# A chunked scan feeding routed experts on one core: TensorE's work of a pair regrouped by form of product, decays brought to C's rows by DMA, routing steps dealt out

## The chip, the cores and the metric

The kernel runs on one core of a Trainium2 chip. The metric is the time of one launch on the device in microseconds (us); lower is better. All arithmetic is 32-bit floating point, partly in TensorE's format fp32r.

## What is computed

Three layers follow each other; y below stands for what one hands to the next.

```python
# 1. a scan over the sequence: batch 4, 8 heads, 768 positions, 32 values, state of 16, in chunks
CB = einsum('bhin,bhjn->bhij', C, B); L = exp(cum_i - cum_j), lower triangle     # cum: running sum of log a
y  = einsum('bhij,bhjd->bhid', CB * L, x) + einsum('bhin,bhnd->bhid', C, state) * exp(cum_i)
state = exp(sum log a) * state + sum_j B_j x_j * exp(cum_end - cum_j)
# 2. routed experts on the rows y (4 x 768 rows of 256, 8 experts of 256 -> 1024 -> 256)
logits = y @ w_gate; fresh = argmax(logits); local = sigmoid(y @ w_local)
e[s] = fresh[s] if s == 0 or local[s] < 0.5 else e[s - 1]        # a recurrence along the sequence
out = softmax(logits)[e] * (relu(y @ w1[e]) @ w2[e])
# 3. a mixer: real part of a 2-D Fourier transform, a residual, a norm, and one more such layer
u = out + real(fft2(out)); result = u + relu(norm(u) @ w_ch1) @ w_ch2
```

## The kernel before

The scan lies in phase_a. The sequence is cut into six chunks of 128 positions, and each chunk into two pairs: a pair is two of the four batches with all eight heads. So the loop over `pairs` makes twelve turns, and a turn i holds parts of pairs i - 1, i and i + 1. The rows of C (ct), transposed B (bt), B (bn) and x of a chunk come by four DMAs in load.

Per pair TensorE makes: scores (L327, g), B's rows against C's rows times the decays, eight products of 128 x 256 whose weights take 32 partitions; the small products of outputs (L355, yps), sixteen with 32 columns of weights each (masked scores times x); the carries (L350, yps), four 128 x 128 products of the state with C's rows; the state's increment (L371, dps) in state_mm; and in rows four transposing products (L409, tl) that turn the pair's result back and take the gate's logits along. Before a chunk's first pair, spread (L258, eb) copies the decays of the heads to the 16 rows of each head by four products with a constant matrix bsel; VectorE then multiplies them into C's rows (ce, L262).

VectorE multiplies the scores by the causal mask (mt, L336: four instructions of 128 x 512 per pair, since a tile g holds one batch and its four banks half used) and dps by a block mask (sn, L380). ScalarE copies finished results from PSUM (x1t, L362 in keep; scr, L412 in rows), scales the state (L396) and C's rows for the scores (ch, L306 in prep). POOL, the GpSimd engine, adds the old state (sn, L386 in state_add), scales x (xt, L314 in prep_x), writes token numbers (L475), and issues the indirect DMAs that scatter finished rows to their experts' places in DRAM (L531 in leave, one for each batch of a chunk).

routing (L414 on) is the gate for a chunk: some 30 small VectorE steps with three short stays on TensorE and ScalarE. It is a generator. Each `yield` ends a step, and three calls put its steps into the order of the engines: gap(n) puts up to n VectorE steps at that place, place(0) and place(1) put the parts that need TensorE. The order is that of the code, since the scheduler is off (`tc.manual_schedule()`); an engine runs its instructions strictly in that order. A chunk's routing is entered once both pairs' rows exist.

Buffers in PSUM: g one tile of four banks, y one bank, m one bank, and the name "t" two banks, which eb, dps and tl take in turn.

In turns 6 to 9 of the loop, the weights of expert 0 are split into two parts: a quarter per turn, ScalarE rounding (L149), VectorE (384 columns) and POOL (640) subtracting (L151, w1l and w2l). load_w issues the loads, which wait on SP for the two raw buffers. After the loop come the last routing, the remaining scatters, the counts and then the experts, the first of which reads its rows (xn) back from DRAM.

## Time and profile before

| what | us |
|---|---|
| three runs | 512.03, 512.13, 513.86 |
| median | 512.13 |
| the profiled execution | 510.82 |
| its span in the profile (first to last instruction) | 509.0 |
| TensorE busy in it | 476.9 (94%) |
| VectorE, POOL, ScalarE busy in it | 276.0, 208.5, 193.0 |
| mean granted clock of TensorE, as a share of full speed | 0.955 |

The span is cut into stretches below: for each, the time that an engine was busy in it and in brackets its instructions, then the granted clock (PEclk, 1.00 is 2.4 GHz, 0.50 is 1.2 GHz), then the mean busy share of the 16 DMA engines and what they moved. In a timeline a row is an instruction or several alike in succession: its start, its length, engine, line of the code, operation, output and inputs by the program's names, and in square brackets how long the engine stood idle before it and on whom it waited. PEld is the loading of weights into TensorE, which goes on beside products. On a chain of waits the rows follow each other in time, each with the stretch of it that set the end.

### The profile page before, as it was taken

Reading aid. Unit: us, or ns where it says so; the run is one execution under the profiler, and the core shown is the slowest. Engines: PE = TensorE matmul, PEld = TensorE weight load, DVE = VectorE, ACT = ScalarE, POOL = GpSimd, SP = SyncE. Lnnn points to the kernel's source line nnn. Section 1 sums busy time; section 2 is a strip of 40 time slices with the busy share of each in tenths; the row PEclk is TensorE's granted clock in tenths of the full one; section 3 lists DMA queues with packets and bytes.
Section 4 is the critical chain, followed back from the end, with each engine's and each line's share of the span. In section 5 each row is a group of like instructions: output and inputs, shape, how many; then the busy total and the mean of one; then the engine's idle time right before and its main releaser. Section 6 shows DMA issues by size and latency. Waiting matters only on the chain.

```text
span 509.0 us, 8586 instructions
## 1 busy us (share of the span) xinstructions
PE 476.9 (94%) x3283; PEld 395.5 (78%) x3283; DVE 276.0 (54%) x695; ACT 193.0 (38%) x391; POOL 208.5 (41%) x214
## 2 busy tenths in 40 slices
PE   7899896886799999999999999798999999999997
PEld 3666563553588989898988989366998989898987
DVE  4566567663364546536363533198554757574341
ACT  2344251530355454635545542124333243443130
POOL 2223463746137575573748454274530343220000
PEclk8999795985899999999999999799999999999999
DMA  8967402132215444535445400440032201000001
GB/s 304 248 196 257 133 23 104 45 126 85 85 57 200 153 149 146 170 124 168 132 144 190 144 26 31 152 151 21 1 96 81 95 1 43 1 30 14 31 12 41
DMA packets 33553, 53.55 MB, mean 105 GB/s; under 512 B 3357, under 2 KB 24189, under 8 KB 33504
## 3 DMA queue, kind: packets, MB, share of 16 engines
q1 hardware_dynamic: 30176, 45.13, 27.8%
q0 software_dynamic: 3072, 7.46, 4.2%
q8 instruction: 28, 0.46, 0.4%
q10 hardware_dynamic: 256, 0.34, 0.2%
q14 instruction: 21, 0.17, 0.1%
HBM read 41.19 MB, written 12.77 MB: 106 GB/s over the span
## 4 chain that ended last, share of the span: by engine, by line
PE 80%; DVE 6%; DMA 5%; POOL 3%; issue 3%; ACT 2%; SPq 0%; POOLq 0%; ACTq 0%; DVEq 0%
PE mm L688 30%; PE mm L697 29%; PE yps L355 3%; PE yps L350 3%; PE dps L371 3%; PE g L327 2%; PE tp L709 2%; PE tl L409 2%; PE f L920 2%; DVE ac L492 1%; DVE mt L336 1%; DMA xs_buf<-scr,si 1%; DMA ca<-in_wg_dram 1%; DMA y_tok<-y,ids 1%; DMA z<-y_tok 1%
## 5 line engine op out<-in xcount | busy, mean ns | idle before, releaser
L690 DVE SCALAR_TENSOR_TENSOR hl<-mm,hh 128x512 fp32r<-128x512 f32 x112 | 77.0, 690 | 76.4 <-ACT hh L689 76.4
L689 ACT ACTIVATE hh<-mm 128x512 fp32r<-128x512 f32 x112 | 66.5, 596 | 92.2 <-PE mm L688 92.2
L697 PE MATMUL mm<-w2h,hh 128*128 128x256 f32 x256 | 71.9, 281 | 0.0
L697 PE MATMUL mm<-w2l,hh 128*128 128x256 f32 x256 | 71.3, 279 | 0.0
L697 PE MATMUL mm<-w2h,hl 128*128 128x256 f32 x256 | 71.3, 279 | 0.0
L737 POOL DMA_INDIRECT y_tok<-y,ids x32 | 34.5, 1078 | 52.9 <-ACT y L736 49.4
L697 PE MATMUL mm<-c2h,hh 128*128 128x256 f32 x192 | 54.4, 284 | 0.0
L697 PE MATMUL mm<-c2h,hl 128*128 128x256 f32 x192 | 53.8, 280 | 0.0
L697 PE MATMUL mm<-c2l,hh 128*128 128x256 f32 x192 | 53.8, 280 | 0.0
L688 PE MATMUL mm<-xh,w1h 128*128 128x512 f32 x128 | 51.3, 401 | 0.5 <-ACT xh L711 0.3
L688 PE MATMUL mm<-xh,w1l 128*128 128x512 f32 x128 | 51.1, 399 | 0.0
L151 POOL TENSOR_TENSOR w1l<-r,w1h 128x640 fp32r<-128x640 f32 x16 | 30.3, 1893 | 45.5 <-ACT w1h L149 45.5
L697 PEld LDWEIGHTS mm<-w2l,hh 128*128 128x128 f32 x256 | 48.3, 189 | 0.0
L697 PEld LDWEIGHTS mm<-w2h,hh 128*128 128x128 f32 x256 | 48.2, 188 | 0.0
L697 PEld LDWEIGHTS mm<-w2h,hl 128*128 128x128 f32 x256 | 48.2, 188 | 0.0
L336 DVE TENSOR_TENSOR mt<-g,ca 128x512 f32<-128x512 f32 x48 | 31.7, 684 | 16.7 <-PE g L327 16.7
L688 PE MATMUL mm<-xl,w1h 128*128 128x512 f32 x128 | 40.5, 398 | 0.0
L688 PE MATMUL mm<-xh,c1h 128*128 128x512 f32 x96 | 39.5, 411 | 0.6 <-ACT xh L711 0.6
L688 PE MATMUL mm<-xh,c1l 128*128 128x512 f32 x96 | 38.0, 396 | 0.0
L697 PEld LDWEIGHTS mm<-c2l,hh 128*128 128x128 f32 x192 | 36.2, 188 | 0.1
L697 PEld LDWEIGHTS mm<-c2h,hh 128*128 128x128 f32 x192 | 36.2, 188 | 0.1
L697 PEld LDWEIGHTS mm<-c2h,hl 128*128 128x128 f32 x192 | 36.2, 188 | 0.0
(301 smaller groups left out, 940.2 us busy)
## 6 DMA issues: line engine op xcount, KB each, us to landing
r<-in_w_dram SPq DMA_DIRECT2D x16, 1024.0 KB, 5.5
xn<-xs_buf SPq DMA_DIRECT2D x8, 530.0 KB, 6.7
rawc<-in_wc_dram SPq DMA_DIRECT2D x8, 512.0 KB, 3.7
out_dram<-o SPq DMA_DIRECT2D x24, 128.0 KB, 1.7
z<-y_tok SPq DMA_DIRECT2D x3, 768.0 KB, 6.0
xs_buf<-scr SPq DMA_DIRECT2D x8, 265.0 KB, 10.1
c1h<-in_x_dram SPq DMA_DIRECT2D x4, 512.0 KB, 5.8
xk<-y_tok SPq DMA_DIRECT2D x4, 512.0 KB, 6.8
```

The lines of the kernel that those rows point to most:

```text
L151: eng.tensor_tensor(out=l_[:, x:y], in0=r_[:, x:y], in1=h[:, x:y], op=ALU.subtract)
L327: PE.matmul(out=gp[:, q, 0, :], lhsT=bt[r:r + 32, :], rhs=ch[r:r + 32, u].rearrange("p q i -> p (q i)"), start=True, stop=True,)
L336: V.tensor_tensor(out=m[:, 2 * q:2 * q + 4, :].rearrange("p (b h) i -> p b h i", b=2), in0=gp[:, q:q + 2, 0, :].rearrange("p b (h i) -> p ...
L350: PE.matmul(out=yps[:, u, g, :], lhsT=s_st[bp][:, u, 128 * g:128 * g + 128], rhs=ops[i][0][:, u, :], start=True, stop=False, skip_group_ch ...
L355: PE.matmul(out=yps[32 * h:32 * h + 32, u, g, :], lhsT=xt[:, u, 4 * g + h, :], rhs=m[:, 4 * g + h, :], start=(c == 0), stop=True, skip_gro ...
L371: PE.matmul(out=dps[:, u, :], lhsT=lds[c]["bn"][:, 2 * bp + u, :], rhs=xts[i][:, u], start=True, stop=True)
L409: PE.matmul(out=tl[:, 137 * g:137 * g + 137], lhsT=x1t[:, u, g, :], rhs=ca[:, o:o + 137], start=True, stop=True)
L688: PE.matmul(out=ps, lhsT=w[:, d, f * 128:(f + 1) * 128], rhs=x[:, d, :], start=(k == 0), stop=(k == 5))
L689: A.activation(out=hh[:, f, :], in_=ps, func=ACTF.Relu)
L690: V.scalar_tensor_tensor(out=hl[:, f, :], in0=ps, scalar=0.0, in1=hh[:, f, :], op0=ALU.max, op1=ALU.subtract)
L697: PE.matmul(out=ps, lhsT=h[:, f, t * 128:(t + 1) * 128], rhs=w[:, f, :], start=(k == 0), stop=(k == 23))
L737: w = G.indirect_dma_start(out=y_tok, out_offset=bass.IndirectOffsetOnAxis(ap=ids[:, t:t + 1], axis=0), in_=y, in_offset=None, bounds_chec ...
```

## The change

Six things are changed in phase_a; the experts and the mixer stay as they are.

1. A turn of the loop is written in another order. scores(i + 1) makes all eight products of the next pair, into four tiles g0 to g3 of a bank each (full banks, both batches in one). Then come the sixteen small products of pair i (intra), dps of pair i + 1, the four tl of pair i, and the four carries of pair i + 1, which now open the bank y a turn ahead.
2. VectorE's four masks belong to the next pair, with up to three routing steps behind each (gap(3)), and four more at the turn's end. A chunk's routing may go on in turns of the next one: two entries in `route` ("n", "a") let a routing wait in its generator until its predecessor has set the running expert and the running counts.
3. The decays e_r are written to a DRAM tile e_d once, and for chunks 1 to 5 eight DMAs on SP's queue (load_eb, one for each head) read them back, each to 16 partitions. Of spread's work only a product remains, on POOL. Chunk 0 keeps the products of TensorE (spread0).
4. The constants ca are two tiles, ca and cb; bsel is cut to 32 rows; the two small loads of the gate's weights move from SP to ScalarE's queue; the first loads are reordered; one warming product more ahead and two behind the columns.
5. Ahead of the loop both prep and prep_x run for pairs 0 and 1, and pair 0's state. After the loop all routings still open are stepped in turn, with the scatters between.
6. load_w(1), the loads of expert 1's weights, is called in turn 10 of the scan instead of ahead of the experts.

```diff
-            warm(3)
-            A.dma_start(out=ca[:, 0:CA1], in_=io["ca"][:, 0:CA1])
+            warm(4)
+            A.dma_start(out=ca, in_=io["ca"][:, 0:CA1])
...
-            load(0)
+            load(0, ("ct", "x"))
+            A.dma_start(out=ca[:, CA["w0"][0]:CA["w0"][0] + 9], in_=io["wg"][0:128, :])
+            A.dma_start(out=ca[:, CA["w1"][0]:CA["w1"][0] + 9], in_=io["wg"][128:256, :])
+            load(0, ("bt", "bn"))
+            SP.dma_start(out=cb, in_=io["ca"][:, CA1:CAW])
...
+            def load_eb(c):
+                ebs[c] = ld.tile([128, NB, 128], FP32, tag="eb", name="eb")
+                for h in range(NH):
+                    SP.dma_start(
+                        out=ebs[c][16 * h:16 * h + 16],
+                        in_=e_d[c * NB:(c + 1) * NB, h, :].unsqueeze(0).to_broadcast([16, NB, 128]),
                     )
+
+            def spread(c):
                 ces[c] = wk.tile([128, NB, 128], FP32, tag="ce", name="ce")
-                V.tensor_tensor(out=ces[c], in0=ps0, in1=lds[c]["ct"], op=ALU.mult)
+                G.tensor_tensor(out=ces[c], in0=ebs[c], in1=lds[c]["ct"], op=ALU.mult)
...
+                gp = [pg.tile([128, 2, 2, 128], FP32, tag=f"g{q}", name=f"g{q}") for q in range(4)]
+                for u in range(2):
+                    for q in range(4):
+                        r = 32 * q
+                        PE.matmul(
+                            out=gp[q][:, u].rearrange("p h i -> p (h i)"), lhsT=lds[c]["bt"][r:r + 32, 2 * bp + u, :],
+                            rhs=ch[r:r + 32, u].rearrange("p q i -> p (q i)"), start=True, stop=True,
+                        )
...
                 yield "first"
+                while route["n"] < c:
+                    yield "first"
...
+                while route["a"] != (c, b0):
+                    yield
                 ac = route["acc"]
...
             decays()
+            SP.dma_start(out=e_d.rearrange("(s u) h i -> (u h) s i", s=2), in_=e_r[:, :, 0:128])
+            columns()
+            spread0()
+            warm(2)
+            prep(0)
+            prep_x(0)
+            prep(1)
+            prep_x(1)
+            scores(0)
             load(1)
+            load_eb(1)
             load(2)
+            load_eb(2)
             zfill(0)
             zfill(4)
...
             mask(0, 0)
             kappa0()
+            kappa()
+            state_up(0, state_mm(0))
+            carry(0)
+            spread(1)

             for i, (c, bp) in enumerate(pairs):
+                now[0] += 1
+                more = i + 1 < NP
                 if bp == 0 and c and c + 2 < NC:
                     load(c + 2)
+                    load_eb(c + 2)
+                if i in (4, 10):
+                    ws = load_w(i // 10)
...
+                if more:
+                    scores(i + 1)
+                    mask(i + 1, 3)
+                else:
+                    gap(10)
+                intra(i)
+                keep(i)
                 if i + 2 < NP:
                     prep(i + 2)
                 place(0)
+                state_add(i)
+                if more and pairs[i + 1][0] + 1 < NC:
+                    state_up(i + 1, state_mm(i + 1))
+                rows(i)
+                state_scale(i)
+                if c + 1 == NC:
+                    route_(c, 2 * bp, 2)
+                elif bp:
+                    route_(c, 0, NB)
+                gap(4)
+                place(1)
+                if more:
+                    carry(i + 1)
                 leave()
+                if bp == 1 and c + 2 < NC:
+                    spread(c + 2)
                 if i + 2 < NP:
                     prep_x(i + 2)
                 leave()
                 if 6 <= i <= 9:
                     next(ws, None)

+            while rq:
+                for r in sorted(rq, key=lambda q: q[2]):
+                    step(r)
                 leave(0)
             while scq:
                 leave(0)
```

TensorE's order in one turn, that of chunk 2's first pair (turn 4). In the rows below g are scores, eb the spread of the decays, tl the transposing products, rp the routing's, yps from ce and scr the carries and yps from mt and xt the small products, dps the state's increment. Before:

```order
L327 MATMUL g<-ch,c2h 128x256 x4
L258 MATMUL eb<-e_r,bsel 128x128 x4
L409 MATMUL tl<-ca,x1t 128x137 x4
L497 MATMUL rp<-oh,ca 128x32
L498 MATMUL rp<-ac,ca 128x32
L350 MATMUL yps<-ce,scr 128x128
L355 MATMUL yps<-mt,xt 32x128 x4
L350 MATMUL yps<-ce,scr 128x128
L355 MATMUL yps<-mt,xt 32x128 x4
L327 MATMUL g<-ch,c2h 128x256 x4
L371 MATMUL dps<-xt,c2l 128x256 x2
L350 MATMUL yps<-ce,scr 128x128
```

After (the lines have moved: L343 scores, L376 small products, L393 dps, L431 tl, L365 carries; the numbers in g_558 and the like only keep the tiles apart):

```order
L343 MATMUL g_558<-ch,c2h 128x256
L343 MATMUL g_559<-ch,c2h 128x256
L343 MATMUL g_560<-ch,c2h 128x256
L343 MATMUL g_561<-ch,c2h 128x256
L376 MATMUL yps<-mt,xt 32x128 x16
L474 MATMUL rp<-ca,kd 4x128 x2
L393 MATMUL dps<-xt,c2l 128x256 x2
L431 MATMUL tl<-ca,x1t 128x137 x4
L495 MATMUL rp<-ca,er 128x4
L365 MATMUL yps<-ce,scr 128x128 x4
```

The sixteen small products stand in one row of sixteen, and the carries in one of four, where they stood in alternation; the products eb are gone; the state's product stands ahead of the tl.

VectorE's order in the same turn; mt are the masks, sn the state's increment, and the other small names (rk, kd, si, ls, sx, cand, ex, ff, px) steps of the routing. Before:

```order
L336 TENSOR_TENSOR mt<-g,ca 128x512
L511 TENSOR_REDUCE rk<-ro 128x4
L427 TENSOR_SCALAR kd<-lg 128x4
L515 TENSOR_TENSOR si<-base,rk 128x4
L430 TENSOR_TENSOR ls<-lg,mx 128x32
L336 TENSOR_TENSOR mt<-g,ca 128x512
L517 TENSOR_SCALAR sx<-sx 128x4
L436 SCALAR_TENSOR_TENSOR cand<-ls,ca 128x32
L520 TENSOR_TENSOR ex<-ex,oh 128x32
L439 TENSOR_REDUCE ff<-cand 128x4
L380 TENSOR_TENSOR sn<-dps,ca 128x512
```

After, where two chunks' routings still take turns between the masks:

```order
L452 TENSOR_TENSOR ls<-lg,mx 128x32
L545 TENSOR_SCALAR sx<-sx 128x4
L458 SCALAR_TENSOR_TENSOR cand<-ls,cb 128x32
L352 TENSOR_TENSOR mt<-g_560,ca 128x2x256
L548 TENSOR_TENSOR ex<-ex,oh 128x32
L461 TENSOR_REDUCE ff<-cand 128x4
L550 RECIPROCAL sx<-sx 128x4
L352 TENSOR_TENSOR mt<-g_561,ca 128x2x256
L463 SCALAR_TENSOR_TENSOR kd<-kd,ff 128x4
L553 TENSOR_REDUCE px<-ex 128x4
L555 TENSOR_TENSOR scr<-px,sx 128x4
L402 TENSOR_TENSOR sn<-dps,cb 128x512
```

Three routing steps stand behind each mask now; sn follows the last of the four masks and twelve such steps, of which the first three stand ahead of these rows.

POOL's order in turns 6 to 8, that is from the end of chunk 3's first pair on; DMA xs_buf are scatters, two rows of the list each time, w1l and w2l the split of expert 0's weights, sn the state's addition, xt the scaling of x, COPY the token numbers. Before:

```order
L151 TENSOR_TENSOR w1l<-r_469,w1h 128x640
L386 TENSOR_TENSOR sn<-scr,sn 128x512
L531 DMA xs_buf<-scr,si 24576x265 x2
L475 COPY scr<-ca 128x4
L314 TENSOR_TENSOR xt<-c1h,f_sb 128x512
L531 DMA xs_buf<-scr,si 24576x265 x2
L151 TENSOR_TENSOR w1l<-r_469,w1h 128x640
L386 TENSOR_TENSOR sn<-scr,sn 128x512
L314 TENSOR_TENSOR xt<-c1l,f_sb 128x512
L151 TENSOR_TENSOR w2l<-r_470,w2h 128x640
```

After (L277 is spread's product, L559 the scatters, L408 sn, L329 xt, L152 the split):

```order
L152 TENSOR_TENSOR w1l<-r_554,w1h 128x640
L408 TENSOR_TENSOR sn<-scr,sn 128x512
L559 DMA xs_buf<-scr,si 24576x265 x2
L277 TENSOR_TENSOR ce<-eb,c2h 128x512
L329 TENSOR_TENSOR xt<-c1h,f_sb 128x512
L559 DMA xs_buf<-scr,si 24576x265 x2
L152 TENSOR_TENSOR w1l<-r_554,w1h 128x640
L408 TENSOR_TENSOR sn<-scr,sn 128x512
L499 COPY scr<-cb 128x4
L329 TENSOR_TENSOR xt<-c1l,f_sb 128x512
L152 TENSOR_TENSOR w2l<-r_555,w2h 128x640
```

Between the two pairs of scatters of turn 7 now stand the product ce and xt, where before COPY and xt stood.

## Rows read from the trace of the kernel before

**Rows 1.** Busy time by stretch: start and end, length, engines, clock, DMA.
```profile
31.15:53.47 22.32, 21.60 (x226) 14.47 (x227) 14.55 (x43) 9.93 (x27) 9.91 (x11) 1.00 0.63 207
53.47:65.80 12.33, 10.74 (x84) 7.39 (x85) 7.31 (x26) 2.86 (x7) 3.71 (x4) 0.72 0.35 112
65.80:112.12 46.32, 37.56 (x351) 24.69 (x348) 30.70 (x85) 17.35 (x42) 27.30 (x25) 0.85 0.22 76
132.35:509.00 376.65, 366.88 (x2358) 325.04 (x2358) 199.28 (x447) 149.17 (x280) 152.80 (x154) 0.99 0.27 88
```

**Rows 2.** Chain of waits in an undisturbed turn: start, length, what.
```profile
31.80 1.20 PE tl L409 x8
...
33.22 0.22 PE yps L350 x2
33.45 0.36 PE yps L355 x8
33.80 0.42 PE yps L350 x2
...
34.58 0.64 PE g L327 x8
35.22 1.06 PE dps L371 x4
```

**Rows 3.** Timeline of VectorE: masks, small steps of the routing, and sn.
```profile
62.35 0.69 DVE L336 TENSOR_TENSOR mt<-g,ca 128x512 f32<-128x512 f32 x1 [3.08 <-PE g L327]
62.96 0.18 DVE L511 TENSOR_REDUCE rk<-ro 128x4 f32<-128x32 f32 x1
...
63.35 0.68 DVE L336 TENSOR_TENSOR mt<-g,ca 128x512 f32<-128x512 f32 x1
...
64.40 0.69 DVE L380 TENSOR_TENSOR sn<-dps,ca 128x512 f32<-128x512 f32 x1
```

**Rows 4.** Timeline of all engines from 76 us: counts, POOL's products, TensorE's wait.
```profile
76.09 4.87 DVE L492 TENSOR_TENSOR ac<-ac,oh 128x8 f32<-128x8 f32 x3
...
77.16 1.56 POOL L151 TENSOR_TENSOR w1l<-r,w1h 128x640 fp32r<-128x640 f32 x1
78.65 1.28 POOL L386 TENSOR_TENSOR sn<-scr,sn 128x512 f32<-128x512 f32 x1
...
79.87 1.06 POOL L314 TENSOR_TENSOR xt<-c1l,f_sb 128x512 f32<-128x512 f32 x1
...
81.02 0.64 PE L498 MATMUL rp<-ac,ca 128*128 128x32 f32 x2 [4.51 <-DVE ac L492]
```

**Rows 5.** Groups of lines, pairs 2 to 4: busy us, mean ns | idle before.
```profile
L492 DVE TENSOR_TENSOR ac<-ac,oh 128x8 f32<-128x8 f32 x3 | 0.5, 166 | 0.1
```

**Rows 6.** Chain of waits behind the wait of rows 4.
```profile
82.24 0.59 PE yps L355 x8
...
88.29 0.31 PE yps L350
```

**Rows 7.** Timeline of VectorE: its part of a weight split.
```profile
67.38 0.56 DVE L151 TENSOR_TENSOR w1l<-r,w1h 128x384 fp32r<-128x384 f32 x1 [1.85 <-ACT w1h L149]
```

**Rows 8.** Timeline at the scan's end: last transposing products (PE), last scatters (POOL).
```profile
113.27 1.20 PE L409 MATMUL tl<-ca,x1t 128*128 128x137 f32 x8
...
121.73 0.97 POOL L531 DMA_INDIRECT xs_buf<-scr,si  x1 [0.30 <-DVE px L525]
123.00 0.97 POOL L531 DMA_INDIRECT xs_buf<-scr,si  x1 [0.30 <-issue]
124.28 0.97 POOL L531 DMA_INDIRECT xs_buf<-scr,si  x1 [0.30 <-issue]
```

**Rows 9.** Timeline of TensorE: the first scores.
```profile
9.45 1.12 PE L327 MATMUL g<-ch,c2h 32*128 32x256 f32 x8 [0.64 <-ACT ch L306]
```

**Rows 10.** DMA issues: KB each, median us from issue to landing.
```profile
xs_buf<-scr SPq DMA_DIRECT2D x8, 265.0 KB, 10.1
...
ar<-in_a_dram SPq DMA_DIRECT2D x1, 96.0 KB, 2.6
```

**Rows 11.** Timeline of SP: a load of expert weights.
```profile
78.75 0.38 SPq L135 DMA_DIRECT2D r<-in_w_dram  x1
```

## Prediction made before the changed kernel was run

> **What bounds the kernel now.** I read the stretches first. From 132.35 us on, in the experts and the mixer, TensorE is busy 366.9 of 376.65 us, and the change leaves that program alone [rows 1]. What can move is the 132 us ahead: the scan over twelve pairs and the hand-over. I cut the scan where ScalarE takes up a pair's finished products (x1t): pair 2 at 31.15, pair 5 at 53.47, pair 6 at 65.80, pair 11 at 112.12. The three pairs to 53.47 take 22.32 us with TensorE 97% busy; the six to 112.12 take 12.33 + 46.32 = 58.65 us, with granted clocks of 0.72 and 0.85 [rows 1]. So there are two different stretches: in the first the products themselves bind, in the second something stops them.
>
> The chain of waits shows the first: products in turn, each change between whole-array and 32-column products costing about 0.2 us (0.22 us for a carry product with its weights ahead, 0.42 behind the small ones) [rows 2]. The timeline shows the second: VectorE's three counts (ac) take 4.87 us where one takes 0.17 in pairs 2 to 4, while POOL runs three products back to back; TensorE stands 4.51 us [rows 4, 5]. Behind that wait the eight small products take 0.59 us instead of 0.36, so TensorE is at the lower of its levels (1.2, not 2.4 GHz), up to 88.29 [rows 2, 6].
>
> **What a turn costs afterwards.** The new order per turn is: eight scores of the next pair, sixteen small products, two state products (dps), four tl, four carries. One wait decides it. The banks "t" are two, and dps, tl, tl take them in turn, so the second tl gets the bank of the next pair's dps and waits until VectorE has made sn from it. VectorE makes sn behind four masks and the routing steps dealt between them. In a turn of a chunk's first half: the first mask starts 0.95 us in (four scores 0.64, one more 0.16, 0.15 to start, an estimate from [rows 2]); four masks at 0.61; twelve small steps at 0.10 (four stand in the 0.39 us between 62.96 and 63.35); sn 0.69 [rows 3]. That is 0.95 + 2.44 + 1.17 + 0.69 = 5.25. Then the second half of tl 0.60, a route product of about 0.2 (an estimate, a carry's price), and four carries at 0.22 [rows 2]: 6.9 us. In the second half six small steps stand there, not twelve, and the route's products come earlier: 4.67 + 0.60 + 0.88 = 6.2 us. So the removed spread products of TensorE, and what the grouping saves it, are worth only what this wait leaves. For pairs 3 to 5 that is 6.9 + 6.2 + 6.9 = 20.0 against 22.3: **-2.3 us**.
>
> **The stretch with scatters and weight splits.** POOL gets one more product per chunk, C's rows times the decays. The trace has no such product; sn (1.28) and xt (1.06) of the same size bound it [rows 4], and I take 1.2. It stands with xt between two pairs of scatters, in the second half of a chunk. VectorE's steps with both inputs in SBUF (counts, oh, si) now stand between the masks, and by [rows 4] one of them can wait for the whole row of POOL products; masks and sn read PSUM and don't. Turn by turn, at the durations above and scatters of 1.28 us each [rows 8]:
> Turn 5: the counts fall on spread and xt, +1.8: 8.0. Turn 6: POOL is through in time: 6.9. Turn 7: the split's ScalarE half now stands behind the evictions and the state's scaling, so VectorE's 0.56 us part, which waited for ScalarE before too [rows 7], starts 1.65 us into the turn; then oh waits for POOL's split (w1l) and sn: 9.65. Turn 8: POOL comes 2.6 us late from its scatters, and si waits behind split, sn and xt: 11.9. Turn 9: split and sn: 8.4. Turn 10: split: 8.65. The last pair has no scores ahead of it: -1.2. Together 52.3 us. TensorE stands 3.9 us in turn 7 and 5.9 in turn 8, both near the 4.51 after which the clock was lower [rows 4]. One such fall costs: 81.02 to 88.29 is 7.3 us for products that take 0.22 + 0.36 + 0.42 + 0.36 + 0.64 + 1.06 + 0.42 + 0.36 and some 0.4 for the route, 4.2 in all, at the other level [rows 2, 6]: 3.05. I count one; the other's turn waits for VectorE anyway. So 55.35 against 58.65: **-3.3 us**. The bounds: without any block 40.1 (-18.5), with both falls 58.4 (-0.25).
>
> On this the Trainium skill has a rule that speaks against the change (SBUF — State Buffer, section "Who interferes with whom"): a VectorE instruction with two SBUF inputs contends with a GpSimd instruction that reads SBUF, and the later one blocks until the earlier finishes. The trace agrees that they block, but shows the wait going over three POOL products; by the page's one instruction it would have ended after at most 1.56 us. What the sum would be by it is the first rival.
>
> **The start.** ScalarE's queue now carries both small weight loads behind ca, ahead of its table load, so the decays are ready some 0.5 us later; two more warm products and the transpositions stand ahead, and the first score comes at about 11.7 us, not 9.45 [rows 9]. Then three turns by the same steps, the first with kappa's product behind pair 0's masks, bring pair 2's x1t to 29.7 against 31.15: **-1.45 us**. The decays take a new way: to DRAM, and back by eight broadcasts for each chunk; POOL must have chunk 1's by about 19. The program issues a queue's DMA only when the eighth before it has landed, so the last broadcast goes out at about 13.6, behind 1.25 MB of chunk 1. At the 2.6 us of the 96 KB load it lands in time, with 3 us to spare; at the zero fill's 10.1 [rows 10] at 23.7, and the term is about +3. I take the first, since the size (32 KB) is nearer to it. SP's queue carries these 40 issues ahead of chunk loads, the zero fill (which moves back some 9 us) and expert 0's weights; all of these are wanted tens of us later, so nothing in the sum. Lower bound of the term -4 (a clock at the upper level from the first score).
>
> **The tail.** From the end of the last tl to the start of the last scatter is now 124.28 - 114.47 = 9.8 us [rows 8]. Afterwards the routing of chunk 4 isn't finished ahead of it: its last step stands 18 VectorE rows behind the last pair's lg, some 3.7 us after tl (1.0 for the evictions, 2.7 for rows that wait on a route product and ScalarE). Then eight scatters at 1.28: the last starts 3.7 + 7 x 1.28 = 12.7 after tl. That is +2.9; the last tl itself follows its x1t 0.5 us sooner, since no route product stands between: **+2.35 us**. Before, eight scatters stood in those 9.8 us too, but their first waited for nothing of the last tl.
>
> **Expert 1's weights.** On SP these loads stand behind rix and ahead of xn in both programs, and the trace issues the first at 78.75, in the scan already [rows 11]. This part does nothing: 0. Smaller edits (bsel, the split constant tile, the decay rows' layout) sit in the start's term.
>
> **Sum.** -1.45 - 2.3 - 3.3 + 2.35 = -4.7 us. Beside the profiled execution (510.82, span 509.0) that is 506.1; that execution lies 1.3 under the median of 512.13, so **507.4 us**.
>
> **Rivals.** (1) A block ends with the POOL instruction in progress: turns 5, 7, 8 and 9 give back 1.05, 1.3, 2.55 and 1.3, so 46.1, and TensorE's stands are too short for a fall: -12.55 in that stretch, -13.95 in all, 498.2. For it: other counts of the same form ran at 0.17 [rows 5]. Against it: [rows 4]. Chance 0.18. (2) Nothing is left: both falls count (58.4) and the start gains nothing: 0 - 2.3 - 0.25 + 2.35 = -0.2, 511.9. For it: the gain hangs on one wait of VectorE per turn, and POOL is fuller than before. Chance 0.20. (3) Slower: the blocks in turns 6 to 9 are each as dear as pair 6 is now, 12.33 us with its fall [rows 1]. Then 8.0 + 4 x 12.33 + 8.65 - 1.2 = 64.75, +6.1, and +4.7 in all: 516.8. It turns to a loss when these four turns average over 11.15 us; mine average 10.0 with the fall. For it: spread lengthens POOL's rows just there. Against it: VectorE's masks of a pair are now a turn ahead of their products, so a block up to about 0.8 us costs nothing. Chance 0.20.
>
> **How the numbers follow.** Forecast 0.42. What a measurement of this kernel can tell from no change is about 0.5%, 2.6 us. Faster: forecast and rival 1, 0.60; same: rival 2, 0.20; slower: rival 3, 0.20. The range takes in rivals 1 and 2, the start's bounds and most of what lies between 511.9 and rival 3; some 0.08 lies under 497 (no block at all) and 0.12 over 515.5.
>
> **What would show it.** Pair 2's x1t near 29.7; in turns 2 to 4, 6 to 7 us each and the second tl waiting for sn; in turns 7 and 8 an oh or si of over 2 us beside POOL's split and sn, TensorE idle before the route's product, and the lower clock behind it; the last scatter some 12.7 us after the last tl. I am wrong if TensorE waits for POOL's ce or the broadcasts, if turns 5 to 9 show no long small step, or if the experts' part moves.

## The result, and the profile after

| | us |
|---|---|
| before, median of 4 runs | 513.0 |
| after, median of 4 runs (518.51 to 521.06) | 519.81 |
| ratio, 95% interval | 1.0129 (1.0088 to 1.017) |
| profiled execution after, and its span | 519.84, 518.0 |

The change makes the kernel 1.3% slower; 507.4 us and a gain were forecast. The stretches of the changed kernel, cut where the prediction cut them (x1t of pairs 2, 5 and 11, then the first expert's first product), answer to [rows 1]:

```profile
29.72:57.58 27.86, 20.52 (x214) 16.19 (x214) 16.20 (x46) 10.04 (x28) 11.56 (x12) 0.88 0.84 233
57.58:116.87 59.29, 42.07 (x407) 33.69 (x407) 36.37 (x112) 21.73 (x51) 33.17 (x32) 0.80 0.32 106
116.87:140.01 23.14, 12.61 (x51) 7.36 (x50) 6.05 (x52) 3.29 (x11) 8.04 (x9) 0.78 0.30 100
140.01:518.00 377.99, 367.08 (x2358) 325.14 (x2358) 197.96 (x447) 149.13 (x280) 153.71 (x154) 0.99 0.27 88
```

| stretch | before | after | difference | forecast |
|---|---|---|---|---|
| start to x1t of pair 2 | 31.15 | 29.72 | -1.43 | -1.45 |
| pairs 2 to 5 | 22.32 | 27.86 | +5.54 | -2.3 |
| pairs 5 to 11 | 58.65 | 59.29 | +0.64 | -3.3 |
| to the first expert's product | 20.23 | 23.14 | +2.91 | +2.35 |
| experts and mixer | 376.65 | 377.99 | +1.34 | 0 |

The sum is +9.0 us, the difference of the two spans. Of the 13.7 us between the forecast (-4.7) and the trace, 7.8 lie in the three turns from pair 2 to pair 5, where TensorE ran at the upper level before (1.00 in [rows 1]); there its mean granted clock is 0.88 now. 6.2 of the 7.8 are turn 4 alone, from pair 4's x1t (44.51) to pair 5's (57.58): 13.1 us, where 6.9 were forecast. The experts and mixer, which the change leaves alone, took between 375.14 (e9) and 378.27 us (e7, e8) in the profiled executions of all the kernels below, so their +1.34 tells nothing of the change. The waits of TensorE in the two stretches (line, what it waited for: us in total, times, the longest), first from 29.72 to 57.58, then from there to 116.87:

```profile
PE rp L474 <- DVE kd L463: 5.0, 2, 4.0
PE tl L431 <- DVE sn L402: 0.8, 2, 0.4
...
PE rp L474 <- DVE kd L463: 8.1, 3, 3.6
PE rp L525 <- DVE ac L519: 4.0, 3, 1.7
PE rp L524 <- DVE oh L505: 2.2, 2, 1.1
```

The wait on which the forecast was built, the second tl for sn, is there and is short: 0.8 us in two places. What stands in the way is another: the first product of a routing, the transposition of kd (L474), which waits for VectorE and stands on TensorE ahead of dps. Turn 4 shows it whole (timeline of all engines; rows of other work left out):

```profile
43.39 0.69 DVE L352 TENSOR_TENSOR mt<-g,ca 128x512 f32<-128x512 f32 x1 [1.10 <-PE g L343]
43.48 1.28 POOL L277 TENSOR_TENSOR ce<-eb,c1l 128x512 f32<-128x512 f32 x1 [8.76 <-PE g L343]
...
44.00 0.18 DVE L539 TENSOR_REDUCE rk<-ro 128x4 f32<-128x32 f32 x1
44.09 0.69 DVE L449 TENSOR_SCALAR kd<-lg 128x4 f32<-128x4 f32 x1
...
45.73 1.28 POOL L408 TENSOR_TENSOR sn<-scr,sn 128x512 f32<-128x512 f32 x1
...
45.85 1.21 DVE L458 SCALAR_TENSOR_TENSOR cand<-ls,cb 128x32 f32<-128x32 f32 x1
...
47.11 1.04 POOL L329 TENSOR_TENSOR xt<-c1h,f_sb 128x512 f32<-128x512 f32 x1
47.58 0.61 DVE L548 TENSOR_TENSOR ex<-ex,oh 128x32 f32<-128x32 f32 x1
...
48.87 0.15 DVE L463 SCALAR_TENSOR_TENSOR kd<-kd,ff 128x4 f32<-128x4 f32 x1
...
49.08 0.37 PE L474 MATMUL rp<-ca,kd 128*4 128x128 f32 x1 [3.96 <-DVE kd L463]
...
49.24 1.98 PE L393 MATMUL dps<-xt,c2l 128*128 128x256 f32 x4
```

Read from the bottom: dps takes 1.98 us instead of the 1.06 of [rows 2], so TensorE is at its lower level (granted clock 0.50 from 49 to 54 us), after standing 3.96 us. It stood for kd, whose last step (48.87) lies behind all four masks and nine dealt steps. And three of those steps (kd 0.69, cand 1.21, ex 0.61) are long because POOL runs ce, xt, sn and xt in a row from 43.48 to 48.15: cand ends at 47.06, as sn ends at 47.01.

POOL's row begins so late because ce waits for the broadcast decays, though the profile names TensorE's g there, which was no input of ce. SP's queue shows the eight broadcasts of chunk 3, a lump of 8.61 us:

```profile
32.85 8.61 SPq L270 DMA_DIRECT2D eb<-e_d  x8
```

The last of them goes out at 41.2 and lands 2.1 us later, at about 43.3; ce starts at 43.48. e9 below tests it.

Where no product of POOL is near, the wait for kd is shorter, but there. Turn 6, timeline of TensorE:

```profile
65.50 0.27 PE L474 MATMUL rp<-ca,kd 128*4 128x128 f32 x1
68.07 0.27 PE L474 MATMUL rp<-ca,kd 128*4 128x128 f32 x1 [2.29 <-DVE kd L463]
...
69.55 2.37 PE L431 MATMUL tl<-ca,x1t 128*128 128x137 f32 x8
```

Four masks and ten short steps, of which kd's is the last, end that late even where nothing holds them up. tl then takes 2.37 instead of the 1.20 of [rows 2]: the clock fell here as well (0.59 from 67.9 to 72).

The tail: 8 scatters follow the last tl, the last at 131.68, 12.96 us after tl's end at 118.72 (9.8 before, [rows 8]). VectorE's last row numbers (si) also wait for a scatter, since si has two buffers and a third routing is in flight:

```profile
117.52 1.20 PE L431 MATMUL tl<-ca,x1t 128*128 128x137 f32 x8 [0.22 <-ACT x1t L384]
...
128.92 0.16 DVE L543 TENSOR_TENSOR si<-base,rk 128x2 int32<-128x2 f32 x1 [3.64 <-DMA xs_buf<-scr,si]
...
131.68 0.98 POOL L559 DMA_INDIRECT xs_buf<-scr,si  x1 [0.30 <-issue]
```

### The profile page after: what moved, and what is told of

The parts are those of the page before. It is cut to its first block, busy times and chain, and to the rows that moved or that the text cites. A ratio compares the mean times of both kernels' runs of the same rounds, so it can differ in the third digit from the quotient of the medians.

```text
span 518.0 us, 8544 instructions
## 1 busy us (share of the span) xinstructions
PE 466.1 (90%) x3247; PEld 397.6 (77%) x3247; DVE 273.3 (53%) x690; ACT 193.9 (37%) x391; POOL 215.4 (42%) x219
## 4 chain that ended last, share of the span: by engine, by line
PE 77%; DVE 11%; DMA 4%; issue 3%; ACT 2%; POOL 2%; SPq 0%; POOLq 0%; DVEq 0%; ACTq 0%
PE mm L695 30%; PE mm L704 29%; DVE mt L352 3%; PE tl L431 3%; PE tp L716 2%; PE dps L393 2%; PE g L343 2%; PE f L926 2%; PE wps L209 2%; PE yps L365 2%; PE cps L940 1%; DMA y_tok<-y,ids 1%; DMA xs_buf<-scr,si 1%; DMA z<-y_tok 1%; DMA xn<-xs_buf 1%
## 5 line engine op out<-in xcount | busy, mean ns | idle before, releaser
L152 POOL TENSOR_TENSOR w1l<-r,w1h 128x640 fp32r<-128x640 f32 x16 | 30.6, 1912 | 45.9 <-ACT w1h L150 45.9
```

The costliest lines, as they stand in the source:

```text
L152: eng.tensor_tensor(out=l_[:, x:y], in0=r_[:, x:y], in1=h[:, x:y], op=ALU.subtract)
```

## The experiments

My theory after the comparison (A): the loss is TensorE standing at kd's transposition, ahead of dps, because the routing steps were dealt between the masks; each such stand also lowers the clock behind it. Rivals: VectorE simply has too much to do per turn (B); POOL's new product ce makes the loss alone (C); the late broadcasts make it (D). And each part of the change has its own price.

All kernels were timed beside runs of before on the same chip. The result, e1 to e4, e5 to e8 and e9 to e11 are four sets, with medians of before of 513.0, 513.41, 514.47 and 516.18 us; between kernels of different sets the ratios are the safer comparison.

| kernel | median us | ratio to before, 95% interval |
|---|---|---|
| changed kernel | 519.81 | 1.0129 (1.0088 to 1.017) |
| e4_weights_only (before + part 6) | 512.41 | 1.0086 (1.0027 to 1.0145) |
| e3_spread_pe (changed, part 3 undone) | 517.6 | 1.0083 (1.0053 to 1.0112) |
| e1_route_behind_rows | 511.3 | 0.9947 (0.9923 to 0.9971) |
| e2_steps_behind_sn | 505.84 | 0.986 (0.979 to 0.993) |
| e6_alternating (e2, grouping undone) | 519.53 | 1.0121 (1.0085 to 1.0156) |
| e9_one_dma | 516.59 | 1.004 (1.0003 to 1.0076) |
| e5_carry_between | 504.01 | 0.9842 (0.9748 to 0.9937) |
| e7_tail | 499.34 | 0.969 (0.9604 to 0.9775) |
| e8_tail_spread_pe | 501.73 | 0.9794 (0.9713 to 0.9874) |
| e10_tail_one_dma | 502.03 | 0.9735 (0.9664 to 0.9805) |
| e11_route_behind_dps | 497.3 | 0.9662 (0.9609 to 0.9716) |

### Expert 1's weights alone (e4)

```diff
-                if i == 4:
-                    ws = load_w(0)
+                if i in (4, 10):
+                    ws = load_w(i // 10)
...
-            ws = load_w(1)
             xn = load_x(pools, 0)
```

> The kernel before with one part of the change, load_w(1) called in turn 10 of the scan. All theories: the loads stand at the same place in SP's queue, nothing moves, 511 to 515 us, ratio 1.00. A ratio clear of 1.00 would show that the call does more than the order of the queue tells.

Measured: the median lies 1.0 us below that of the runs of before beside it (513.41), while the ratio lies above 1; the runs of before beside it spread from 505.35 to 517.12, and the two measures disagree, so I go by the trace. It is 2.23 us late at pair 2's x1t already (33.38), 2.42 at the load of expert weights ([rows 11]: 78.75, here 81.17) and 2.63 at pair 11's x1t (114.75): the shift is made in the start, eight turns ahead of the edit. There the same eight products run at the lower level in this execution, where they ran at the upper one in that of before (one row each, e4 first):

```profile
13.48 1.91 PE L258 MATMUL eb<-e_r,bsel 32*128 32x128 f32 x8
```

```profile
13.39 1.05 PE L258 MATMUL eb<-e_r,bsel 32*128 32x128 f32 x8
```

So this part does nothing, as forecast; between these two executions of the same first turns the clock of the start alone made some 2 us.

### The spread back on TensorE (e3)

```diff
-                G.tensor_tensor(out=ces[c], in0=ebs[c], in1=lds[c]["ct"], op=ALU.mult)
+                ps0 = pg.tile([128, NB, 128], FP32, tag="t", name="eb", bufs=2)
+                for b in range(NB):
+                    PE.matmul(out=ps0[:, b, :], lhsT=bsel[r:r + 32, b, :], rhs=e_r[r:r + 32, q, 0:128], ...)
+                V.tensor_tensor(out=ces[c], in0=ps0, in1=lds[c]["ct"], op=ALU.mult)
```

> The changed kernel with part 3 undone: the decays of all chunks are spread by TensorE's products, and VectorE multiplies them from PSUM into C's rows, no DMA broadcast and no product on POOL. Theory A (POOL's additional product makes the row of POOL products longer that VectorE's steps wait for, one of several in that row): turn 4's wait for kd falls from 4.0 to about 2.7 us, TensorE's clock may hold there, 514 to 518 us. Theory C (the product on POOL alone makes the loss): the waits for kd go and the time is that of the kernel before or less, 503 to 512 us.

Measured: 517.6, inside theory A's range, and the waits for kd are still there. From 29 to 118 us:

```profile
PE rp L480 <- DVE kd L469: 9.5, 5, 2.7
```

The longest is 2.7 instead of 4.0, and the turn from pair 4 to 5 takes 8.7 us instead of 13.1, though other turns are longer. As the only cause, theory C falls: without any product of POOL for the decays TensorE still stands at kd, and the kernel is still slower than before. But the product has a share. In the profiled execution pairs 2 to 11 take 81.98 us, 5.2 less than in the changed kernel, though TensorE makes the spread again; in return pair 2's x1t comes at 32.67, 2.95 us later. So part 3 pays in the start and costs in the scan.

### The route's first product behind the transposing ones (e1)

```diff
-                place(0)
                 state_add(i)
...
                 rows(i)
+                place(0)
                 state_scale(i)
```

> The changed kernel with one edit: the first route product of a turn, place(0), is written behind rows instead of behind keep, so that on TensorE the state's increment and the transposing products go ahead of it. Theory A (the loss is TensorE standing at the route's transposition of kd, 5.0 us in 2 waits from 29.72 to 57.58 us and 8.1 in 3 from there to 116.87, plus the lower clock behind each): those waits shrink to under 1 us each, the pairs 2 to 11 take some 70 to 75 us instead of 87.2, and the whole takes 503 to 509 us. Theory B (VectorE's long turn binds whatever stands where on TensorE, since sn lies behind the same steps): the wait moves to the second tl, waiting for sn, and the time stays at 515 to 520.

Measured: 511.3. That is 8 us under the changed kernel, but 2 over theory A's range; pairs 2 to 11 take 79.87 us, where it gave 70 to 75, and 4.0 us of waits for kd are left in three places. Turn 2 shows why:

```profile
33.08 0.73 PE L431 MATMUL tl<-ca,x1t 128*128 128x137 f32 x4 [2.11 <-DVE sn L402]
...
35.01 0.26 PE L495 MATMUL rp<-ca,er 4*128 4x4 f32 x1 [0.97 <-DVE er L491]
35.20 2.08 PE L365 MATMUL yps<-ce,scr 128*128 128x128 f32 x8
```

Here the wait moved to the second tl and to er, the next that hang on VectorE, and the clock fell behind them (carries 2.08 instead of 1.16 in e2 at the same place). Both theories have a share: the position on TensorE costs, and so does what stands ahead of sn on VectorE. The next run takes that away.

### The routing steps behind sn (e2)

```diff
-                    mask(i + 1, 3)
+                    mask(i + 1, 0)
...
-                gap(4)
+                gap(16)
                 place(1)
```

> The changed kernel with the routing steps taken out from between the masks (0 instead of 3 behind each) and up to 16 put behind sn at the turn's end. The same steps run, and TensorE's order is untouched. Theory A (a step held up by POOL between two masks delays kd, for which TensorE stands ahead of dps): kd is ready before the turn begins, the waits for kd go, 500 to 508 us. Theory B (VectorE has too much to do per turn wherever the steps stand): the next turn's masks and sn come late instead, TensorE waits at the small products or at tl, 514 to 520 us.

Measured: 505.84, inside theory A's range; no step is fewer, and TensorE's order is the changed kernel's. From pair 2 to pair 11 it takes 69.86 us (87.15 in the changed kernel, 80.97 before), and the waits for kd are down to 1.6 us in three places (16.1 in nine in the changed kernel, both halves of kd counted). So theory B falls: VectorE has time for these steps, it is their place that costs. What remains is the block beside POOL, now at a later step (timeline, turn 7):

```profile
71.56 2.85 DVE L519 TENSOR_TENSOR ac<-ac,oh 128x8 f32<-128x8 f32 x1
...
72.07 1.30 POOL L277 TENSOR_TENSOR ce<-eb,c2h 128x512 f32<-128x512 f32 x1
73.31 1.06 POOL L329 TENSOR_TENSOR xt<-c1h,f_sb 128x512 f32<-128x512 f32 x1
...
74.89 0.42 PE L525 MATMUL rp<-ac,cb 128*128 128x32 f32 x1 [3.99 <-DVE ac L519]
```

One count waits over both products, as in [rows 4], and TensorE stands 3.99 us for it. Its tail is longer, 25.16 us from pair 11's x1t to the first expert's product, since chunk 4's routing ends later still and si waits 3.35 us.

### Grouping by form undone (e6)

```diff
                 for u in range(2):
                     for g in range(2):
+                        if c:
+                            PE.matmul(out=ys[i][:, u, g, :], lhsT=s_st[bp][:, u, 128 * g:128 * g + 128], ...)
                         for h in range(4):
...
-                    carry(i + 1)
```

> The kernel with the steps behind sn (e2) with one part of the change undone: carries and small products of a pair alternate again as before (one carry, four small products, four times), instead of four carries a turn ahead and sixteen small products in a row. If grouping by form is worth what the changes of form cost (0.22 to 0.42 for a carry in alternation against 0.26 in a row, and 0.36 for four small against 0.25), some 0.6 us in each of ten turns: 509 to 513 us against 505.8. If TensorE's time is not what sets the turn, 504 to 508.

Measured: 519.53, 13.7 us over e2, more than the 3 to 7 that were expected. One alternation in e6 (a carry, four small products), and the small products in a row and the carries in a row in e2, at the upper level:

```profile
35.80 0.49 PE L365 MATMUL yps<-ce,scr 128*128 128x128 f32 x2
36.22 0.42 PE L370 MATMUL yps<-mt,xt 128*32 128x128 f32 x8
```

```profile
34.63 1.16 PE L365 MATMUL yps<-ce,scr 128*128 128x128 f32 x8
...
36.80 1.08 PE L376 MATMUL yps<-mt,xt 128*32 128x128 f32 x32
```

Four alternations run from 35.80 to 38.89, 3.09 us; in e2 carries and small products take 1.09 and 1.01 to the next row's start, 2.10. That is 1.0 us in each of ten turns. The rest goes with the clock (mean granted 0.84 from pair 2 to 11, in e2 0.90): TensorE is busy 68.53 us there, in e2 55.90, while the time that it isn't busy is about the same (14.3 and 14.0). So grouping by form is worth over 10 us in e2's order. What it is worth in the changed kernel itself, with its waits, no run shows.

### One broadcast per chunk (e9)

```diff
-                for h in range(NH):
-                    SP.dma_start(out=ebs[c][16 * h:16 * h + 16],
-                        in_=e_d[c * NB:(c + 1) * NB, h, :].unsqueeze(0).to_broadcast([16, NB, 128]))
+                SP.dma_start(out=ebs[c].rearrange("p u i -> p (u i)"),
+                    in_=e_d[c].rearrange("h u i -> h (u i)").unsqueeze(1).to_broadcast([NH, 16, NB * 128]))
```

> The changed kernel with the broadcast of the decays made by one DMA per chunk (256 KB) instead of eight of 32 KB; the decays are written to DRAM chunk by chunk, in an order that makes this possible. Theory D (in the changed kernel chunk 3's eight broadcasts were issued from 32.85 to 41.46 us and landed at about 43.4, so POOL's row ce, xt, sn, xt began at 43.48 and lay over turn 4's routing steps): ce of chunk 3 starts at 38 to 41.5, turn 4's wait for kd falls from 4.0 to about 2.4 us, pairs 2 to 11 take 82 to 84 us instead of 87.2, 514 to 517 us. Theory A alone (the wait hangs on kd behind masks and steps, the DMA doesn't matter): ce may start earlier, the wait stays at 3.5 or more, 518 to 521 us.

Measured: 516.59, 3.2 us under the changed kernel (ratio 1.004 instead of 1.0129), in theory D's range. Turn 4 again, POOL and TensorE:

```profile
39.37 1.27 POOL L280 TENSOR_TENSOR ce<-eb,c1l 128x512 f32<-128x512 f32 x1 [5.67 <-PE tl L434]
```

```profile
46.61 0.27 PE L477 MATMUL rp<-ca,kd 128*4 128x128 f32 x1 [2.25 <-DVE kd L466]
46.72 1.09 PE L396 MATMUL dps<-xt,c2l 128*128 128x256 f32 x4
```

ce starts 4.1 us sooner, POOL's row is through by 44.0, the wait for kd is 2.25 instead of 3.96, and dps runs at the upper level. The turn from pair 4 to 5 takes 9.9 us instead of 13.1. So the late broadcasts were a cause, for this turn; the 2.25 that are left are theory A's. From pair 2 to 11 it still takes 85.92 us, above the 82 to 84 expected and only 1.2 under the changed kernel: later turns gave most of it back. The larger part of the gain in the profiled execution, 2.85 us, lies in the experts and mixer (375.14), which this edit doesn't touch. So that the time fell into theory D's range is in part luck, and what the broadcasts cost the whole kernel isn't shown.

### Towards a faster kernel (e5, e7, e8, e10, e11)

e5 builds on e2: the carries fill the gap between the two halves of tl, steps go where VectorE waits for scores, a chunk's last steps go ahead of rows.

```diff
+                gap(7)
                 if more:
                     scores(i + 1)
...
-                rows(i)
+                gap(10)
+                rows(i, lambda: more and carry(i + 1))
                 state_scale(i)
...
-                gap(16)
+                gap(8)
                 place(1)
-                if more:
-                    carry(i + 1)
```

> The kernel with the steps behind sn (e2), and three moves more: the four carries of the next pair stand between the two halves of tl, so that they fill the wait for sn; up to 7 routing steps stand ahead of a turn's masks, where VectorE waits for scores; the last steps of a chunk stand ahead of rows. In e2 TensorE waited 4.9 us in seven places for sn and 6.9 us in six for the counts (ac). Theory A (what is left are waits for VectorE that hang on where its steps stand): both go below 2 us, pairs 2 to 11 take 60 to 64 us instead of 69.9, 497 to 502 us. Theory B (POOL's rows decide): the counts still wait beside POOL's split and ce, one wait of 3 us or more remains with the lower clock behind it, 503 to 507 us.

Measured: 504.01, which is theory B's side: the waits for sn fell from 4.9 to 2.3 us, but a count still waits 3.0 us beside POOL, and a first product waits 3.3 for a step (ls). Pairs 2 to 11 take 72.22 us, more than e2's 69.86 and far from theory A's 60 to 64; the intervals of e5 and e2 overlap, so no gain over e2 is shown.

e7 adds four buffers for si, chunk 4's routing at the last turn's start and VectorE's part of a split behind the masks.

```diff
-                si = sm.tile([128, nb], I32, tag="si", name="si")
+                si = sm.tile([128, nb], I32, tag="si", name="si", bufs=4)
...
                 else:
-                    gap(10)
+                    place(0)
+                    gap(12)
+                    leave(0)
+                    leave(0)
```

> e5 with the scan's end changed and the splits moved: four buffers for the scatters' row numbers (si) instead of two, since VectorE's last si waited 3.64 us in the changed kernel and 3.35 us in e2 for a scatter that still read an older one; chunk 4's routing finished at the last turn's start, its scatters asked for ahead of the last tl; VectorE's part of a split behind the masks of the next turn instead of ahead. Theory A: from the last x1t to the first expert's product 20 to 22 us, instead of 25.2 in e2, and the whole 3 to 5 us less than e5. Theory B (POOL's queue of scatters is the bound there in any case, 1.28 us each): 1 us less than e5 or nothing.

Measured: 499.34, 4.7 less than e5. The end, from pair 11's x1t (99.38) to the first expert's product (121.43), takes 22.05 us, just outside the 20 to 22 of theory A; in e5 it took 22.96, so most of the difference lies elsewhere. In this kernel the state's increment of turn 4 waited for xt, which stood behind ce and its broadcast:

```profile
PE dps L395 <- POOL xt L331: 3.4, 1, 3.4
```

e8 is e7 with e3's edit, the spread on TensorE.

> e7 with the decays spread by TensorE and VectorE as before, without DMA broadcast and POOL product. If POOL is what turns 4 to 9 wait for (its load is some 14 us in two turns with a split and four scatters), this is 2 to 4 us less than e7; if TensorE is, its additional 1.15 us per chunk makes it 2 to 5 us more; the later first x1t (21.22 instead of 18.83 in the single undo) adds up to 2.

Measured: 501.73, 2.4 more than e7, with an interval that overlaps e7's: where the decays are spread makes no difference to the whole that these runs can tell. The profiled executions show e3's trade again: pair 2's x1t 2.8 us later (32.38), pairs 2 to 11 4.6 us shorter (65.25). e10 is e7 with e9's edit, one broadcast.

> e7 with the one broadcast DMA per chunk. In e7 the state's increment of turn 4 waited 3.4 us for xt, which stood on POOL behind chunk 3's ce, and that waited for its broadcast until 44.53. Theory D: this wait goes, with the lower clock behind it 5 us less, 493 to 496 us. Otherwise 498 to 501.

Measured: 502.03, neither the 493 to 496 of theory D nor the 498 to 501 without it. The wait of dps for xt is gone and the turn from pair 4 to 5 takes 8.7 us instead of 11.9, but the next takes 13.4 instead of 5.0. There VectorE's base (one small step) waits over three products of POOL, and TensorE 2.93 us for the counts behind it:

```profile
48.63 4.16 DVE L515 TENSOR_SCALAR base<-f__621 128x4 f32<-128x4 f32 x1
...
49.26 1.28 POOL L413 TENSOR_TENSOR sn<-scr,sn 128x512 f32<-128x512 f32 x1
...
50.48 1.27 POOL L282 TENSOR_TENSOR ce<-eb,c1l 128x512 f32<-128x512 f32 x1
51.70 1.05 POOL L334 TENSOR_TENSOR xt<-c1h,f_sb 128x512 f32<-128x512 f32 x1
```

The gain was given back one turn later. e11 is e10 with the routing's first product behind dps.

```diff
-                place(0)
                 state_add(i)
                 if more and pairs[i + 1][0] + 1 < NC:
                     state_up(i + 1, state_mm(i + 1))
+                place(0)
```

> e10 with the first route product of a turn behind the state's increment instead of ahead of it. In e7 TensorE waited 9.3 us there in nine places for kd and ls. Theory A: the 1.0 us of the increment covers part of each, 2 to 4 us less than e10. Against it: VectorE's ro and the scan er then come later, and TensorE waits for er at the turn's end; then the same as e10 within 2 us.

Measured: 497.3, 4.7 less than e10, where theory A gave 2 to 4, and 3.4% under before. It has the lowest median of all, though e7's interval overlaps its own. Its stretches, pairs 2 to 11 and the tail:

```profile
29.11:95.76 66.65, 51.94 (x625) 41.37 (x624) 57.81 (x165) 31.39 (x79) 43.56 (x41) 0.96 0.55 176
95.76:117.34 21.58, 14.25 (x46) 8.21 (x44) 5.33 (x42) 3.20 (x11) 8.36 (x10) 0.73 0.34 115
```

The granted clock is 0.96 in the scan, where it was 0.72 and 0.85 in the two disturbed stretches before [rows 1] and 0.88 and 0.80 in the changed kernel. The tail is 1.35 us longer than before; nothing of the gain comes from it.

## Why the prediction was wrong, step by step

**The step that failed** is "One wait decides it", the second tl for sn. sn was where it was forecast, behind four masks and twelve steps. But the order shown ahead of the prediction had another product between the small products and dps: rp from kd, and kd is the tenth of those twelve steps. I counted the route's products as 0.2 us of TensorE and not as places where it waits. TensorE stood there 1.0 us in turn 2, 2.3 in turn 6, where nothing held the steps up, and 4.0 in turn 4, where POOL did; dps, sn, tl and the next turn's start came that much later. Forecast for the turns to pair 5: 20.0; measured 27.86. e1 and e2 show the cause from both sides, with 7.3 and 17.3 us off pairs 2 to 11. e1 also shows that the forecast's own wait is the next behind it: once rp was out of the way, the second tl stood 2.11 us for sn.

**Blocks in the quiet turns.** I let steps wait beside POOL from turn 5 on only, where scatters and splits are. But POOL's row of ce, xt, sn, xt exists in turn 4 too, and it was late there by the broadcasts. I had priced only chunk 1's broadcasts, and had put at nothing only what their issues delay; for the later chunks' own there was no term. Chunk 3's were wanted at about 39 (e9's ce) and ce started at 43.48. In e9 this turn is 3.2 us shorter, and the six turns from pair 5 on are 2.9 us longer.

**The stretch with scatters and splits.** From x1t to x1t the six turns took 8.1, 9.7, 10.2, 13.2, 8.7 and 9.3 us, where turns 5 to 10 were forecast at 8.0, 6.9, 9.65, 11.9, 8.4 and 8.65 - 1.2, and 3.05 for one fall of the clock. That steps wait beside POOL was right, and so was the worst turn, 8; how they wait was not. The prediction looked for an oh or si of over 2 us in turns 7 and 8. In turn 7 each held-up step ends with the one POOL product in progress, and the next step waits for the next product:

```profile
74.24 1.92 POOL L152 TENSOR_TENSOR w1l<-r,w1h 128x640 fp32r<-128x640 f32 x1 [9.70 <-ACT w1h L150]
...
75.27 0.94 DVE L505 TENSOR_TENSOR oh<-cb,f__840 128x32 f32<-128x32 f32 x1
...
76.12 1.26 POOL L408 TENSOR_TENSOR sn<-scr,sn 128x512 f32<-128x512 f32 x1
76.12 1.28 DVE L508 TENSOR_SCALAR base<-f__840 128x4 f32<-128x4 f32 x1
```

Turn 8 goes the same way with kd, ls and cand (0.82, 0.66 and 1.10, against split, sn and xt), si takes 0.15, and TensorE stands 1.27 and 3.64 us for kd, not at the counts. So rival 1 had the way a block ends here, but not that TensorE's stands would be too short for a fall. Mis-sized were turn 6, which has the unblocked wait for kd and its clock, and turn 10: I took 1.2 off for missing scores, but the wait for kd stood in their place (2.16 us).

**The clock.** One fall was counted; in the trace the level is the lower one behind the waits for kd in turns 4, 6, 8 and 10 (dps or tl there take about twice their time), and also behind the waits for counts in turns 7 (granted clock 0.63 from 78.4 to 83) and 9 (0.55 from 102.6 to 106.4). Theory A's "each such stand" goes too far: behind the 1.0 us of turn 2 the clock held (1.00 up to 43.48).

**The sum's bound.** By the prediction's own turns of 6.2 and 6.9 us, less 1.2, the stretch without any block is 38.1 us, not 40.1. The forecast doesn't hang on it.

**What held.** The start (29.72 against 29.7), with some luck: in e1, e2 and e5 pair 2's x1t came at 28.89 to 30.35, and in e4 the clock alone moved it by some 2 us; the tail (last scatter 12.96 us after tl, forecast 12.7), to which si's wait added 0.4; expert 1's weights (nothing); the worth of grouping was called "worth only what this wait leaves", and e6 shows it is over 10 us in e2, where most of the waits for kd are gone. POOL's product took 1.28, 1.2 was taken.

**The rivals.** The time (519.81) lies above rival 3 (516.8), whose mechanism, dear blocks turn after turn, came nearest, but its place was turns 6 to 9, and more than half of the miss was made in turns 2 to 4. None of the rivals had TensorE stand at kd. The range ended at 515.5.

## What to carry to other kernels

When steps of a side task are dealt into the gaps of one engine, go through the order of the engine that consumes them and find the first instruction there that needs a dealt step: all that stands behind it waits with it, however small it is. Put the steps behind the last result that the main chain needs, and let the consumer stand one piece of independent work later. A transfer whose consumer stands on an engine that blocks another is on the path through that engine's order, even if nothing waits for it directly.

## What the runs showed of the hardware

A VectorE step with a single input in SBUF waits beside POOL as well. e10's base (one input of 128 x 4, its rows above) takes 4.16 us from 48.63 and ends at 52.79, as xt, the last of POOL's three products, ends at 52.75. In the changed kernel's turn 4 the single-input kd (0.69) ends at 44.78, as ce ends at 44.76, while the reduction rk, 0.09 us ahead of it and beside the same ce, takes 0.18. The prediction had only steps with two such inputs. The Trainium skill (SBUF — State Buffer, section "Who interferes with whom") says both: tensor_scalar can take the ports that VectorE shares with GpSimd, and tensor_reduce on trn2 never contends. It also says that the later instruction blocks until the earlier one finishes; the rows of e2, e10 and [rows 4] show waits that go on over the next POOL products, while kd, cand and ex in the changed kernel's turn 4 and oh and base in its turn 7 end with the product in progress. What decides between the two, these runs leave open; POOL's whole uninterrupted row is the upper bound of a block that they show.

The length of a stand alone doesn't tell whether TensorE's level falls. After 2.25 us in e9's turn 4 the next products ran at the upper level (dps 1.09); after 2.29 us in the changed kernel's turn 6 tl ran at the lower one (2.37 for eight). What decides between these two is open as well.
